# Late attention scores as three 64-row products on the two row halves of TensorE, with ScalarE and VectorE in written order

## The chip, the cores and the metric

The kernel runs on one core of one Trainium2 chip. The metric is the device time of that core in microseconds (us), from start to end of one launch. The time before is 664.21 us, the median of three runs (664.04 to 664.49). One execution was also taken with a profile; the rows shown below are from that execution.

## What is computed

Attention with a banded and a global part, and then a two-layer block that works on each token. There are 4 batches, 8 heads, 768 positions and 64 elements per head. A query looks at the 96 keys that end at itself and at the first 8 keys of the sequence; both limits come as inputs.

```python
scores = scale * np.matmul(q, k.transpose(0, 1, 3, 2))
...
scores = scores + bias[None, :, :, :]          # -slope of the head times distance
scores = np.where(keep, scores, -1000000000.0)
scores = scores - np.max(scores, axis=-1, keepdims=True)
a = np.exp(scores)
a = a / (np.sum(a, axis=-1, keepdims=True) + 1e-09)
return np.matmul(a, v).astype(np.float32)
...
h = x @ w_in                                   # 3072 x 512 by 512 x 2048
relu6 = np.clip(h + 3.0, 0.0, 6.0)
g = h * relu6 / 6.0
return (g @ w_out).astype(np.float32)
```

## The kernel before, in words

**Blocks, pairs, tiles.** The 3,072 tokens are cut into 8 blocks of 384 (two to a batch). A block has 3 tiles of 128 queries, and its 8 heads are handled as 4 pairs. For a tile only 232 keys matter (96 before the tile, 8 global ones, the 128 of the tile); the first tile of a sequence has 128. The attention of the first three blocks (12 pairs, `EARLY`) is done ahead, in an early part; from block 2 of the second layer on, the attention of block i+1 is woven into the two-layer work of block i. "Late" means those 5 blocks, 20 pairs and 60 tiles.

**The two-layer block.** It is done in three products of rounded parts: a high and a low part of each operand, in a 32-bit matmul type of one pass (`F32R`), leaving out low times low. Per step `f` (16 to a block) `first` (L179) issues 12 products of 384 columns, `gate` makes g (ScalarE L190, VectorE L191), `high` rounds it (GpSimd L197 in the late part), `rest` makes the low part (VectorE L204), and `second` (L211) issues 9 products of 512 columns for the step before. `halves` (L448) yields once after each `first` and once after each `second`, so a block has 32 places, called units here, at which attention work is put in. Even units lie behind `first` and `gate`, odd units behind `second`.

**A late pair before.** `attention` (L630) fills the units. Counted from the pair's first unit: units 0, 1 and 2 hold the scores of tiles 0, 1 and 2; unit 3 the first step of `split` for the pair after it, `sum_up` and `normalize` of tiles 0 and 1; unit 4 `normalize` of tile 2, `spread` of tile 0 and the second step of `split`; unit 5 the last two `spread`, `fetch` and the third step of `split`. A pair takes 6 units. After every second pair, at its unit 11, `values` (L917) is issued for both pairs.

- `split` (L783) makes the parts of queries and keys. For each head, q is loaded on both row halves; ScalarE makes the high part q1 (L797), VectorE the low part q2 (L801); GpSimd writes the high part of k on the head's own half (L798) and VectorE the low part of k on the other half (L804). So a tile `kx` holds high over low on 128 rows.
- `scores` (L809) issues for each head two products of 128 rows (L827), q1 on kx and q2 on kx: four products to a tile, into one PSUM bank. In the early part (`plain`, L823) the two heads stand on the two row halves, each with products of 64 rows, and each head has a bank of its own.
- `score` (L841, VectorE) adds distances and takes the minimum; `weigh` (L848, ScalarE) makes exponentials and sums; `sum_up` (L855, L856) and `normalize` (L865, GpSimd) divide.
- `spread` (L890) turns 32 x 32 blocks on VectorE and writes them to DRAM (L892), `fetch` (L899) reads them back turned, both on SyncE's queue. `values` multiplies the weights by v in products with 64 columns of the array (L917).

**What sets the order.** TensorE, SyncE and GpSimd are held in the written order to the end (`in_order`, L565). ScalarE and VectorE are held in it through the early part alone (L541); in the late part the framework's scheduler orders them, by a model of times of its own.

**Memory.** `load` (L298) brings keys and queries of a pair in one transfer and its values in another, into two rooms used in turn. The late scores take their banks in turn from two pools (`bank`, L241).

**The end.** `doubt` (L335) reduces the least scores on VectorE, transposes the result on TensorE (L342) and sets a flag; it is put at unit 4 of the last block.

Of the kernel before, what the change touches and what calls it, by code (L numbers as in the profile page):

```python
# [9 lines left out]
F32 = mybir.dt.float32  # L10
F32R = mybir.dt.float32r
I32 = mybir.dt.int32
U32 = mybir.dt.uint32
AF = mybir.ActivationFunctionType
ALU = mybir.AluOpType
PSUM = bass.MemoryType.PSUM

B, H, S, D = 4, 8, 768, 64
DM, DF = 512, 2048
P = 128  # L20
NT = 3
TB = NT * P
# [11 lines left out]
QW = 2 * TB  # L34
VW = 2 * NT * P
LOAD = KW + QW + VW
# [8 lines left out]
BOTH = EARLY  # L45
# [15 lines left out]
class Kernel:  # L61
# [36 lines left out]
    def constants(self):  # L98
        nc = self.nc
        self.const = self.pool("const", 1)  # L100
        self.ident = self.const.tile([P, P], F32, name="ident")
        make_identity(nc, self.ident)
        self.small = self.const.tile([P, 3], F32, name="small")
        self.little = self.const.tile([P, 2 * NT], F32, name="little")
        nc.vector.memset(self.little, 1e-9)
        self.three = self.small[:, 0:1]
        nc.vector.memset(self.three, 3.0)
# [126 lines left out]
    def attending(self, ctx, heads, rows, ps, **kw):  # L234

        if heads:
            self.hp = self.pool("hp", heads, ctx=ctx, **kw)
        self.up = self.pool("up", rows, ctx=ctx, **kw)
        self.tp = self.pool("tp", ps, ctx=ctx, **kw)
# [58 lines left out]
    def load(self, n, values):  # L298

        if n < len(self.blocks) * NPAIR:  # L300
            end = KW + (TB if n < BOTH else QW)
            for columns in (slice(KW + QW, LOAD),) if values else (slice(0, KW), slice(KW, end)) if n == 0 else (slice(0, end),):
                self.nc.sync.dma_start(out=self.place(n)[:, columns], in_=self.pairs[n, :, columns])
# [8 lines left out]
    def loaded(self, n):  # L312


        at = self.place(n)
        q = at[:, KW:KW + QW].rearrange("p (j t c) -> p j t c", j=2, t=NT)
        v = at[:, KW + QW:LOAD].rearrange("p (s t c) -> p s t c", s=2, t=NT)
        return at[:, 0:KW], q, v[:, 0], v[:, 1]
# [15 lines left out]

    def doubt(self, flag):  # L335


        nc = self.nc
        one = self.small[:, 2:3]
        nc.vector.tensor_reduce(out=one, in_=self.least, op=ALU.max, axis=mybir.AxisListType.X)  # L340
        row = self.bank("t")
        nc.tensor.transpose(row[0:1, 0:P], one, self.ident)  # L342
        top = self.small[0:1, 1:2]
        nc.vector.tensor_reduce(out=top, in_=row[0:1, 0:P], op=ALU.max, axis=mybir.AxisListType.X)
        nc.vector.tensor_scalar(out=flag, in0=top, scalar1=LOW, scalar2=self.beyond(), op0=ALU.is_ge, op1=ALU.max)
# [148 lines left out]
    def banded(self, flag):  # L494
# [12 lines left out]
        with ExitStack() as early, ExitStack() as words:  # L507
# [11 lines left out]
            with ExitStack() as ctx:  # L519
                self.room += self.rooms(self.pool("more", 1, ctx=ctx), MORE - ROOMS, ROOMS)  # L520
                self.load(2, False)
                for n in range(ROOMS):
                    self.load(n, True)
                self.plain_distances(ctx)
                self.attending(ctx, 0, 9, 5)
                pairs = [Pair(self, n, xs[n // NPAIR], True) for n in range(EARLY)]
                todo = self.halves([(0, f, xs[0], acc) for f in range(FIRST)])
                for n in range(-2, EARLY + 1):
                    self.ahead(n, pairs, acc, todo)
                for _ in todo:  # L530
                    pass
# [9 lines left out]
            self.in_order(start, mybir.EngineType.Activation, mybir.EngineType.DVE)  # L541
        self.attending(self.ctx, 2, 3, 2, side="right")
        self.bp = self.pool("bp", 2, side="right")
        self.there = self.pool("there", 2, bass.MemoryType.DRAM)
        self.score_banks = 2
        self.op = self.pool("op", 3, side="right")
        x, ahead = xs[2], None
        for i in range(2, len(self.blocks)):
            units, x_next = [], None
            if i + 1 < len(self.blocks):  # L550
                x_next = self.x_tiles()
                units, ahead = self.attention(i + 1, x_next, ahead)
                if i == 2:
                    units = [[]] + units
            else:
                units = [[]] * 4 + [[lambda: self.doubt(flag)]]
            acc = self.acc_tiles()
            steps = [(i, f, x, acc) for f in range(NF)]
            for k, _ in enumerate(self.halves(steps if x_next else steps[:-3], True)):
                for unit in units[k] if k < len(units) else ():  # L560
                    unit()
            if not x_next:
                self.end(steps[-3:])
            x = x_next
        self.in_order(start, mybir.EngineType.PE, mybir.EngineType.SP, mybir.EngineType.Pool)  # L565
# [64 lines left out]
    def attention(self, i, x, first):  # L630
# [8 lines left out]
        for p in range(NPAIR):  # L639
# [4 lines left out]
            for t in range(NT):  # L644
                at[t].append(lambda t=t, me=me: me.scores(t)())
            if after:
                at[3].append(lambda after=after: after.split(0))
            at[3] += [me.sum_up, lambda me=me: me.normalize(0), lambda me=me: me.normalize(1)]
            at[4] += [lambda me=me: me.normalize(2), lambda me=me: me.spread(0)]
            at[5] += [lambda me=me: me.spread(1), lambda me=me: me.spread(2), me.fetch]  # L650
            for t in range(1, NT if after else 0):
                at[t + 3].append(lambda t=t, after=after: after.split(t))
            if p % 2 == 1:
                at[11] += [lambda me=pairs[p - 1]: me.values("x"), lambda me=me: me.values("s")]
# [113 lines left out]
class Pair:  # L768
# [4 lines left out]
    def __init__(self, kernel, n, x, plain):  # L773
        self.k, self.nc, self.n, self.x, self.plain, self.both = kernel, kernel.nc, n, x, plain, n < BOTH
# [3 lines left out]
        self.parts = [{}, {}]  # L778
# [4 lines left out]
    def split(self, step, load=True):  # L783
# [5 lines left out]
        for j, part in enumerate(self.parts):  # L789
            h = 2 * self.pr + j  # L790
            scale = float(-1.0 / (np.sqrt(D) * SLOPES[h]))
            own, other = (slice(0, D), slice(D, P)) if j == 0 else (slice(D, P), slice(0, D))
            if step == 0:
                part["q1"] = kk.hp.tile([P, NT, P], F32R, name="q1")
                part["q2"] = kk.hp.tile([P, NT, P], F32R, name="q2")
                part["kx"] = kk.hp.tile([P, KW], F32R, name="kx")
                nc.scalar.mul(out=part["q1"], in_=q[:, j], mul=scale)  # L797
                nc.gpsimd.tensor_scalar(out=part["kx"][own, c], in0=k[own, c], scalar1=1.0, scalar2=0.0,  # L798
                                        op0=ALU.mult, op1=ALU.add)
            elif step == 1:  # L800
                nc.vector.scalar_tensor_tensor(out=part["q2"], in0=q[:, j], scalar=scale, in1=part["q1"].bitcast(F32),  # L801
                                               op0=ALU.mult, op1=ALU.subtract)
            else:
                nc.vector.tensor_tensor(out=part["kx"][other, c], in0=k[own, c], in1=part["kx"][own, c].bitcast(F32),  # L804
                                        op=ALU.subtract)
        if step == 2 and load:
            kk.load_next(self.n, False)

    def scores(self, t):  # L809
# [3 lines left out]
        if t != 1 or not self.both:  # L813
            self.banks = [kk.bank("s")[:, 0:2 * W].rearrange("p (i c) -> p i c", i=2) for _ in range(2 if self.both else 1)]
        sp = [self.banks[j][:, t % 2] if self.both else self.banks[0][:, j] for j in range(2)]
# [4 lines left out]
        for j in range(2):  # L820
            if self.plain:
                rows, q = (slice(j * D, (j + 1) * D), 0) if self.both else (slice(None), j)
                nc.tensor.matmul(sp[j][:, lo:W], lhsT=queries[rows, q, t], rhs=keys[rows, c], start=True, stop=True)  # L823
            else:
                part = self.parts[j]
                for m, q in enumerate((part["q1"], part["q2"])):
                    nc.tensor.matmul(sp[j][:, lo:W], lhsT=q[:, t], rhs=part["kx"][:, c], start=(m == 0), stop=(m == 1))  # L827
# [113 lines left out]
def pair_loads(q, k, v):  # L941
# [8 lines left out]
    for b in range(B):  # L950
        for a in range(0, S, TB):
            cols = np.concatenate([np.arange(a - PREV, a).clip(0)]
                                  + [np.concatenate([np.arange(NG), np.arange(p, p + P)]) for p in range(a, a + TB, P)])
            for h in range(0, H, 2):
# [3 lines left out]
                for j in range(2):  # L958
                    for half in range(2):
                        if n >= EARLY or half == j:  # L960
                            column = KW + (j * TB if n >= BOTH else 0)
                            at[half * D:(half + 1) * D, column:column + TB] = qt[j, :, a:a + TB]
                vt = v[b, h:h + 2].transpose(1, 0, 2).reshape(S, P)
                va = at[:, KW + QW:].reshape(P, 2, NT, P)
# [3 lines left out]
                at[:, KW + QW:] = va.reshape(P, VW)  # L968
# [31 lines left out]
```

## Time and profile before

| | |
|---|---|
| median of three runs | 664.21 us |
| profiled execution | 664.76 us |
| its span, first to last instruction | 662.9 us |
| mean granted TensorE clock | 0.999 |
| TensorE busy | 652.2 us, 98% |
| VectorE, ScalarE, GpSimd busy | 402.6, 271.8, 231.5 us |
| late part, 202 to 600 us | TensorE busy 397.63 of 398.00 us |

PE is the row of matmuls and PEld that of weight loads, which run beside the matmuls. The time of a matmul in the trace runs to its modelled end, while the next one has already begun; what a product takes from TensorE is therefore read as the distance from its start to the next start. In the chain of waits, each piece of the span is put down to the work that held up the end. A row of the timeline has the start, the length of the piece, engine, line, operation, output and inputs, shape (rows x columns of the array used, then rows x moving columns) and the count of like instructions that were merged.

### The profile page before, as it was taken

Reading aid. Unit: us, or ns where it says so; the run is one execution under the profiler, and the core shown is the slowest. Engines: PE = TensorE matmul, PEld = TensorE weight load, DVE = VectorE, ACT = ScalarE, POOL = GpSimd, SP = SyncE. Lnnn points to the kernel's source line nnn. Section 1 sums busy time; section 2 is a strip of 40 time slices with the busy share of each in tenths; the row PEclk is TensorE's granted clock in tenths of the full one; section 3 lists DMA queues with packets and bytes.
Section 4 is the critical chain, followed back from the end, with each engine's and each line's share of the span. In section 5 each row is a group of like instructions: output and inputs, shape, how many; then the busy total and the mean of one; then the engine's idle time right before and its main releaser. Section 6 shows DMA issues by size and latency. Waiting matters only on the chain.

```text
span 662.9 us, 11223 instructions
## 1 busy us (share of the span) xinstructions
PE 652.2 (98%) x3963; PEld 582.1 (88%) x3963; DVE 402.6 (61%) x1028; ACT 271.8 (41%) x702; POOL 231.5 (35%) x389
## 2 busy tenths in 40 slices
PE   9989999999999999999999999999999999999997
PEld 8767888888889999899989989899998989989995
DVE  6887677777745776367654777357663677432222
ACT  6998545444445343244314333143422444121111
POOL 4787333333202533034331454134340444312110
PEclk9999999999999999999999999999999999999999
DMA  7975433333003566526652456615654256510001
GB/s 237 314 240 186 150 128 126 120 119 117 29 1 135 147 168 172 149 88 163 172 150 96 122 149 183 176 55 143 163 140 127 88 146 155 130 48 2 0 1 53
DMA packets 58530, 84.32 MB, mean 127 GB/s; under 512 B 8160, under 2 KB 45280, under 8 KB 56416
## 3 DMA queue, kind: packets, MB, share of 16 engines
q1 hardware_dynamic: 58176, 83.25, 42.2%
q8 instruction: 33, 0.54, 0.3%
q14 instruction: 33, 0.27, 0.1%
q10 hardware_dynamic: 288, 0.26, 0.1%
HBM read 62.52 MB, written 20.97 MB: 126 GB/s over the span
## 4 chain that ended last, share of the span: by engine, by line
PE 92%; ACT 4%; DMA 2%; issue 1%; DVE 0%; POOL 0%; SPq 0%; POOLq 0%; ACTq 0%
PE hp L179 40%; PE acc L211 34%; PE xp L917 3%; ACT n L848 2%; PE sp L827 2%; PE sp L211 2%; PE tp L917 2%; PE tp L211 2%; PE xp L211 2%; PE tp L827 2%; PE xp L371 1%; DMA there<-blocks 1%; ACT pt L877 1%; PE sp L823 1%; DMA weights<-there 1%
## 5 line engine op out<-in xcount | busy, mean ns | idle before, releaser
L190 ACT ACTIVATE g<-hp,small 128x384 f32<-128x384 f32 x127 | 73.6, 580 | 254.2 <-PE hp L179 225.8
L179 PE MATMUL hp<-xh,w1h 128*128 128x384 f32 x512 | 173.5, 339 | 0.3 <-DVE pt L877 0.3
L179 PE MATMUL hp<-xh,w1l 128*128 128x384 f32 x512 | 172.6, 337 | 0.0
L179 PE MATMUL hp<-xl,w1h 128*128 128x384 f32 x512 | 171.9, 336 | 0.0
L197 POOL TENSOR_SCALAR gh<-g 128x384 fp32r<-128x384 f32 x96 | 51.6, 537 | 293.9 <-DVE g L191 259.4
L211 PE MATMUL acc<-w2h,gl 128*128 128x512 f32 x336 | 132.8, 395 | 0.0
L211 PE MATMUL acc<-w2h,gh 128*128 128x512 f32 x336 | 132.2, 394 | 0.1
L211 PE MATMUL acc<-w2l,gh 128*128 128x512 f32 x336 | 132.1, 393 | 0.0
L191 DVE SCALAR_TENSOR_TENSOR g<-g,hp 128x384 f32<-128x384 f32 x128 | 69.8, 545 | 85.1 <-ACT g L190 84.7
L204 DVE TENSOR_TENSOR gl<-g,gh 128x384 fp32r<-128x384 f32 x128 | 77.9, 609 | 67.4 <-POOL gh L197 45.3
L865 POOL TENSOR_SCALAR n<-n,sums 128x232 f32<-128x232 f32 (+1 forms) x186 | 99.2, 549 | 28.2 <-DVE sums L856 13.5
L848 ACT ACTIVATE n<-n,least 128x232 f32<-128x232 f32 (+1 forms) x192 | 89.0, 466 | 42.5 <-DVE least L841 41.9
L179 PEld LDWEIGHTS hp<-xh,w1h 128*128 128x128 f32 x512 | 96.3, 188 | 6.1 <-issue 1.5
L179 PEld LDWEIGHTS hp<-xl,w1h 128*128 128x128 f32 x512 | 96.2, 188 | 3.9
L179 PEld LDWEIGHTS hp<-xh,w1l 128*128 128x128 f32 x512 | 96.1, 188 | 0.0
L211 PEld LDWEIGHTS acc<-w2h,gl 128*128 128x128 f32 x336 | 63.0, 188 | 14.6 <-DVE gl L204 0.6
L211 PEld LDWEIGHTS acc<-w2h,gh 128*128 128x128 f32 x336 | 63.3, 188 | 10.6 <-POOL gh L197 0.6
L211 PEld LDWEIGHTS acc<-w2l,gh 128*128 128x128 f32 x336 | 63.2, 188 | 10.2
L890 DVE STREAM_TRANSPOSE blocks<-n 128x256 f32<-128x256 f32 x112 | 43.5, 424 | 31.4 <-POOL n L865 18.6
L385 POOL TENSOR_SCALAR wst<-wst 128x1024 f32<-128x1024 int32 x16 | 23.7, 1480 | 54.6 <-ACT wz L384 54.5
L841 DVE CUSTOM_DVE_ANT_0 n<-sp,d 128x232 f32<-128x232 f32 (+1 forms) x70 | 23.6, 374 | 30.3 <-PE sp L827 29.1
L798 POOL TENSOR_SCALAR kx<-load 64x504 fp32r<-64x504 f32 (+1 forms) x40 | 31.1, 777 | 19.2 <-PE hp L179 17.6
(116 smaller groups left out, 764.1 us busy)
## 6 DMA issues: line engine op xcount, KB each, us to landing
wst<-w SPq DMA_DIRECT2D x16, 1024.0 KB, 4.8
there<-blocks SPq DMA_DIRECT2D x52, 256.0 KB, 2.6
load<-pairs SPq DMA_DIRECT2D x20, 636.0 KB, 5.2
load<-pairs SPq DMA_DIRECT2D x32, 384.0 KB, 4.3
weights<-there SPq DMA_DIRECT2D x48, 192.0 KB, 3.5
out<-o SPq DMA_DIRECT2D x23, 256.0 KB, 2.2
weights<-there SPq DMA_DIRECT2D x32, 160.0 KB, 3.2
load<-pairs SPq DMA_DIRECT2D x11, 444.0 KB, 4.5
```

What stands on the lines that cost most here:

```text
L179: self.nc.tensor.matmul(hp, lhsT=self.w1(w, f)[:, kt, :], rhs=a[:, kt, :], start=(n == 0), stop=(n == 3 * NKT - 1))
L190: nc.scalar.activation(out=g, in_=hp, func=AF.Relu, bias=self.three, scale=1.0)
L191: nc.vector.scalar_tensor_tensor(out=g, in0=g, scalar=6.0, in1=hp, op0=ALU.min, op1=ALU.mult)
L197: self.nc.gpsimd.tensor_scalar(out=gh, in0=g, scalar1=1.0, scalar2=0.0, op0=ALU.mult, op1=ALU.add)
L204: self.nc.vector.tensor_tensor(out=gl, in0=g, in1=gh.bitcast(F32), op=ALU.subtract)
L211: self.nc.tensor.matmul(acc[tt], lhsT=a[:, tk], rhs=self.w2(w, f), start=(f == 0 and j == 0), stop=(f == NF - 1 and j == 2))
L798: nc.gpsimd.tensor_scalar(out=part["kx"][own, c], in0=k[own, c], scalar1=1.0, scalar2=0.0, op0=ALU.mult, op1=ALU.add)
L827: nc.tensor.matmul(sp[j][:, lo:W], lhsT=q[:, t], rhs=part["kx"][:, c], start=(m == 0), stop=(m == 1))
L848: nc.scalar.activation(out=e[:, j, lo:W], in_=e[:, j, lo:W], func=AF.Exp, bias=self.least[:, i:i + 1], scale=-1.0, accum_out=self.sums[:, ...
L865: nc.gpsimd.tensor_scalar(out=e[:, j, lo:W], in0=e[:, j, lo:W], scalar1=over, scalar2=0.0, op0=ALU.mult, op1=ALU.add)
L890: nc.vector.transpose(out=blocks[:, :, s].rearrange("p b j q -> p j b q"), in_=e[:, :, c:c + P].rearrange("p j (b q) -> p j b q", b=4))
L917: nc.tensor.matmul(xps[j * D:(j + 1) * D, t * P:(t + 1) * P], lhsT=vt[0:K, t, j * D:(j + 1) * D], rhs=self.part(t, j, c, K), start=(c == 0 ...
```

## The change

Both heads of a late pair now stand on the two row halves, as in the early part. q and k are each loaded once; `split` makes q1, q2, k1, k2 with one instruction each over all 128 rows, with a column of factors per pair instead of a number per head. `scores` issues three products per head (q1 k1, q1 k2, q2 k1), each of 64 rows, alternating between the halves, so six products to a tile. Each head has its own bank, shared by tiles 0 and 1. The scores of tiles 0 and 1 are issued together in unit 0, and those of tile 2 in unit 2. The steps of `split` move to units 1, 2 and 3, all of `normalize` goes to unit 3, `values` moves from unit 11 to unit 10. The pool of split parts now holds two pairs. In block 2 the attention starts one unit later. The reduction of `doubt` becomes `worst`, two units ahead of the rest, which moves to unit 6. ScalarE and VectorE are held in the written order to the end.

```diff
-        self.attending(self.ctx, 2, 3, 2, side="right")
+        self.op = self.pool("op", 3, side="right")
+        for h in range(H):
+            self.nc.gpsimd.memset(self.factors[h % 2 * D:(h % 2 + 1) * D, h // 2:h // 2 + 1], float(PLAIN / SLOPES[h]))
+        self.attending(self.ctx, 3, 2, side="right")
         self.bp = self.pool("bp", 2, side="right")
+        self.hp = self.pool("hp", 2, side="right")
...
                 if i == 2:
-                    units = [[]] + units
+                    units = [[], []] + units
             else:
-                units = [[]] * 4 + [[lambda: self.doubt(flag)]]
+                units = [[]] * 4 + [[self.worst], [], [lambda: self.doubt(flag)]]
...
-        self.in_order(start, mybir.EngineType.PE, mybir.EngineType.SP, mybir.EngineType.Pool)
+        self.in_order(start, *(getattr(mybir.EngineType, e) for e in ('PE', 'SP', 'Pool', 'Activation', 'DVE')))
...
-            for t in range(NT):
-                at[t].append(lambda t=t, me=me: me.scores(t)())
+            at[0].append(lambda me=me: [f() for f in [me.scores(0), me.scores(1)]])
             if after:
-                at[3].append(lambda after=after: after.split(0))
-            at[3] += [me.sum_up, lambda me=me: me.normalize(0), lambda me=me: me.normalize(1)]
-            at[4] += [lambda me=me: me.normalize(2), lambda me=me: me.spread(0)]
-            at[5] += [lambda me=me: me.spread(1), lambda me=me: me.spread(2), me.fetch]
-            for t in range(1, NT if after else 0):
-                at[t + 3].append(lambda t=t, after=after: after.split(t))
+                at[1].append(lambda after=after: after.split(0))
+            at[2].append(lambda me=me: me.scores(2)())
+            if after:
+                at[2].append(lambda after=after: after.split(1))
+            at[3].append(me.sum_up)
+            at[3].append(lambda me=me: me.normalize(0))
+            at[3].append(lambda me=me: me.normalize(1))
+            at[3].append(lambda me=me: me.normalize(2))
+            if after:
+                at[3].append(lambda after=after: after.split(2))
+            at[4].append(lambda me=me: me.spread(0))
+            at[5].append(lambda me=me: me.spread(1))
+            at[5].append(lambda me=me: me.spread(2))
+            at[5].append(me.fetch)
             if p % 2 == 1:
-                at[11] += [lambda me=pairs[p - 1]: me.values("x"), lambda me=me: me.values("s")]
+                at[10] += [lambda me=pairs[p - 1]: me.values("x"), lambda me=me: me.values("s")]
...
+        factor = kk.factors[:, self.pr:self.pr + 1]
+        if step == 0:
+            self.q1, self.q2 = (kk.hp.tile([P, NT, P], F32R, name=name) for name in ("q1", "q2"))
+            self.k1, self.k2 = (kk.hp.tile([P, KW], F32R, name=name) for name in ("k1", "k2"))
+            nc.scalar.activation(out=self.q1, in_=q, func=AF.Copy, scale=factor)
+            nc.gpsimd.tensor_scalar(out=self.k1[:, c], in0=k[:, c], scalar1=1.0, scalar2=0.0, op0=ALU.mult, op1=ALU.add)
+        elif step == 1:
+            nc.vector.scalar_tensor_tensor(out=self.q2, in0=q, scalar=factor, in1=self.q1.bitcast(F32), op0=ALU.mult, op1=ALU.subtract)
+        else:
+            nc.vector.tensor_tensor(out=self.k2[:, c], in0=k[:, c], in1=self.k1[:, c].bitcast(F32), op=ALU.subtract)
...
-        for j in range(2):
-            if self.plain:
-                rows, q = (slice(j * D, (j + 1) * D), 0) if self.both else (slice(None), j)
-                nc.tensor.matmul(sp[j][:, lo:W], lhsT=queries[rows, q, t], rhs=keys[rows, c], start=True, stop=True)
-            else:
-                part = self.parts[j]
-                for m, q in enumerate((part["q1"], part["q2"])):
-                    nc.tensor.matmul(sp[j][:, lo:W], lhsT=q[:, t], rhs=part["kx"][:, c], start=(m == 0), stop=(m == 1))
+        products = ((queries, keys),) if self.plain else ((self.q1, self.k1), (self.q1, self.k2), (self.q2, self.k1))
+        for m, (q, k) in enumerate(products):
+            for j in range(2):
+                rows = slice(j * D, (j + 1) * D)
+                nc.tensor.matmul(sp[j][:, lo:W], lhsT=q[rows, t], rhs=k[rows, c], start=(m == 0), stop=(m == len(products) - 1))
```

More of the change, by code (lines that the diff above doesn't have):

```diff
@@ L33 @@
 KW = PREV + NT * TG
-QW = 2 * TB
 VW = 2 * NT * P
-LOAD = KW + QW + VW
+LOAD = KW + TB + VW
 NEG = 1.0e9
@@ L44 @@
 EARLY = AHEAD * NPAIR
-BOTH = EARLY
 ROOMS = 2
@@ L103, in constants @@
         self.small = self.const.tile([P, 3], F32, name="small")
+        self.factors = self.const.tile([P, NPAIR], F32, name="factors")
         self.little = self.const.tile([P, 2 * NT], F32, name="little")
@@ L231, in acc_tiles, with attending @@
         return [self.ps_o.tile([P, BANK], F32, name="acc") for _ in range(NT)]
-    def attending(self, ctx, heads, rows, ps, **kw):
-        if heads:
-            self.hp = self.pool("hp", heads, ctx=ctx, **kw)
+    def attending(self, ctx, rows, ps, **kw):
         self.up = self.pool("up", rows, ctx=ctx, **kw)
@@ L300, in load @@
         if n < len(self.blocks) * NPAIR:
-            end = KW + (TB if n < BOTH else QW)
-            for columns in (slice(KW + QW, LOAD),) if values else (slice(0, KW), slice(KW, end)) if n == 0 else (slice(0, end),):
+            end = KW + TB
+            for columns in (slice(end, LOAD),) if values else (slice(0, KW), slice(KW, end)) if n == 0 else (slice(0, end),):
                 self.nc.sync.dma_start(out=self.place(n)[:, columns], in_=self.pairs[n, :, columns])
@@ L315, in loaded @@
         at = self.place(n)
-        q = at[:, KW:KW + QW].rearrange("p (j t c) -> p j t c", j=2, t=NT)
-        v = at[:, KW + QW:LOAD].rearrange("p (s t c) -> p s t c", s=2, t=NT)
+        q = at[:, KW:KW + TB].rearrange("p (t c) -> p t c", t=NT)
+        v = at[:, KW + TB:LOAD].rearrange("p (s t c) -> p s t c", s=2, t=NT)
         return at[:, 0:KW], q, v[:, 0], v[:, 1]
@@ L333, in distances, with worst @@
                     self.nc.gpsimd.tensor_scalar(out=p[:, h], in0=d, scalar1=c, scalar2=0.0, op0=ALU.mult, op1=ALU.add)
+    def worst(self):
+        self.nc.vector.tensor_reduce(out=self.small[:, 2:3], in_=self.least, op=ALU.max, axis=mybir.AxisListType.X)
     def doubt(self, flag):
         nc = self.nc
-        one = self.small[:, 2:3]
-        nc.vector.tensor_reduce(out=one, in_=self.least, op=ALU.max, axis=mybir.AxisListType.X)
         row = self.bank("t")
-        nc.tensor.transpose(row[0:1, 0:P], one, self.ident)
+        nc.tensor.transpose(row[0:1, 0:P], self.small[:, 2:3], self.ident)
         top = self.small[0:1, 1:2]
@@ L524, in banded @@
                 self.plain_distances(ctx)
-                self.attending(ctx, 0, 9, 5)
+                self.attending(ctx, 9, 5)
                 pairs = [Pair(self, n, xs[n // NPAIR], True) for n in range(EARLY)]
@@ L540, in banded @@
                 self.decode_step()
-            self.in_order(start, mybir.EngineType.Activation, mybir.EngineType.DVE)
-        self.attending(self.ctx, 2, 3, 2, side="right")
+        self.op = self.pool("op", 3, side="right")
+        for h in range(H):
+            self.nc.gpsimd.memset(self.factors[h % 2 * D:(h % 2 + 1) * D, h // 2:h // 2 + 1], float(PLAIN / SLOPES[h]))
+        self.attending(self.ctx, 3, 2, side="right")
         self.bp = self.pool("bp", 2, side="right")
+        self.hp = self.pool("hp", 2, side="right")
         self.there = self.pool("there", 2, bass.MemoryType.DRAM)
         self.score_banks = 2
-        self.op = self.pool("op", 3, side="right")
         x, ahead = xs[2], None
@@ L773, in __init__ @@
     def __init__(self, kernel, n, x, plain):
-        self.k, self.nc, self.n, self.x, self.plain, self.both = kernel, kernel.nc, n, x, plain, n < BOTH
+        self.k, self.nc, self.n, self.x, self.plain = kernel, kernel.nc, n, x, plain
         self.tb, self.pr = kernel.blocks[n // NPAIR][1], n % NPAIR
@@ L777, in __init__ @@
         self.sums, self.rows, self.pts = None, [], []
-        self.parts = [{}, {}]
     def low(self, t):
@@ L788, in split @@
         c = slice(CB if self.tb == 0 else 0, None)
[L789 to L802, printed above, removed]
-            else:
[L804 to L807, printed above, removed]
+        factor = kk.factors[:, self.pr:self.pr + 1]
[8 more added lines that the diff above has]
+            nc.vector.tensor_tensor(out=self.k2[:, c], in0=k[:, c], in1=self.k1[:, c].bitcast(F32), op=ALU.subtract)
+            if load:
+                kk.load_next(self.n, False)
     def scores(self, t):
@@ L812, in scores @@
             self.sums = kk.up.tile([P, 2, 2 * NT], F32, name="sums")
-        if t != 1 or not self.both:
-            self.banks = [kk.bank("s")[:, 0:2 * W].rearrange("p (i c) -> p i c", i=2) for _ in range(2 if self.both else 1)]
-        sp = [self.banks[j][:, t % 2] if self.both else self.banks[0][:, j] for j in range(2)]
+        if t != 1:
+            self.banks = [kk.bank("s")[:, 0:2 * W].rearrange("p (i c) -> p i c", i=2) for _ in range(2)]
+        sp = [self.banks[j][:, t % 2] for j in range(2)]
         e = kk.up.tile([P, 2, W], F32, name="n")
@@ L819, in scores @@
         keys, queries, _, _ = kk.loaded(self.n)
-        for j in range(2):
-            if self.plain:
-                rows, q = (slice(j * D, (j + 1) * D), 0) if self.both else (slice(None), j)
-                nc.tensor.matmul(sp[j][:, lo:W], lhsT=queries[rows, q, t], rhs=keys[rows, c], start=True, stop=True)
-            else:
-                part = self.parts[j]
-                for m, q in enumerate((part["q1"], part["q2"])):
-                    nc.tensor.matmul(sp[j][:, lo:W], lhsT=q[:, t], rhs=part["kx"][:, c], start=(m == 0), stop=(m == 1))
+        products = ((queries, keys),) if self.plain else ((self.q1, self.k1), (self.q1, self.k2), (self.q2, self.k1))
[3 more added lines that the diff above has]
+                nc.tensor.matmul(sp[j][:, lo:W], lhsT=q[rows, t], rhs=k[rows, c], start=(m == 0), stop=(m == len(products) - 1))
         self.rows.append(e)
@@ L957, in pair_loads @@
                 at[:, 0:KW] = kt[:, :, cols].reshape(P, KW)
[L958 to L962, printed above, removed]
+                at[:, KW:KW + TB] = qt[:, :, a:a + TB].reshape(P, TB)
                 vt = v[b, h:h + 2].transpose(1, 0, 2).reshape(S, P)
-                va = at[:, KW + QW:].reshape(P, 2, NT, P)
+                va = at[:, KW + TB:].reshape(P, 2, NT, P)
                 va[:, 0] = vt[a:a + TB].reshape(NT, P, P).transpose(1, 0, 2)
@@ L967, in pair_loads @@
                     va[0:CB, 1, t] = vt[tile_rows(a + t * P)]
-                at[:, KW + QW:] = va.reshape(P, VW)
+                at[:, KW + TB:] = va.reshape(P, VW)
                 n += 1
```

## The prediction

> **What bounds the kernel now.** I read the page's first two parts, then the chain of waits, then the busy time by stage, and last the timeline of TensorE where the change cuts in.
>
> ```profile
> span 662.9 us, 11223 instructions
> PE 652.2 (98%) x3963; PEld 582.1 (88%) x3963; DVE 402.6 (61%) x1028; ACT 271.8 (41%) x702; POOL 231.5 (35%) x389
> PEclk9999999999999999999999999999999999999999
> ```
>
> ```profile
> by line: PE hp L179 39.6%; PE acc L211 34.1%; PE xp L917 3.3%; ACT n L848 2.4%; PE sp L827 2.3%; PE sp L211 1.9%; PE tp L917 1.9%; PE tp L211 1.7%; PE xp L211 1.7%; PE tp L827 1.7%; PE xp L371 1.4%; DMA there<-blocks 0.9%; ACT pt L877 0.7%;
> ```
>
> ```profile
> 202.00:600.00 398.00, 397.63 (x2410) 361.01 (x2409) 241.37 (x654) 141.34 (x398) 139.12 (x240) 1.00 0.49 135
> ```
>
> The last row is the late part; its busy times stand in the order PE, PEld, DVE, ACT, POOL. TensorE (PE) is busy for 397.63 of 398.00 us, and the granted clock is full. Nothing else in the late part is on the path: what shortens TensorE's stream shortens the kernel, and what makes TensorE stand longer between two products lengthens it one for one. The late scores (L827) are 2.3% + 1.7% = 4.0% of the chain, 26.5 us. That is all that the change can work on directly.
>
> **What the old scores cost.**
>
> ```profile
> 439.71 0.34 PE L179 MATMUL hp<-xh,w1l 128*128 128x384 f32 x1
> 439.88 0.60 PE L827 MATMUL sp<-kx,q 128*128 128x232 f32 x4
> 440.32 0.40 PE L211 MATMUL acc<-w2h,gh 128*128 128x512 f32 x1
> 440.56 0.39 PE L211 MATMUL acc<-w2l,gh 128*128 128x512 f32 x1
> ```
>
> Read by starts: four products take 440.32 - 439.88 = 0.44 us, 0.11 us each, and the products before and after them run at their usual distance (0.17 us for 384 columns, 0.24 for 512 here). So the scores enter and leave TensorE's stream at no cost. 60 tiles at 0.44 make 26.4 us, which agrees with the chain's 26.5.
>
> **What the new scores stream.** Six products to a tile, but two at a time on the two row halves. The early part already does this, in plain 32-bit products of two passes each:
>
> ```profile
> 32.70 0.27 PE L873 MATMUL hp<-ident,n 128*128 128x128 f32 x1
> 32.81 0.27 PE L875 MATMUL hp<-ident,n 128*128 128x128 f32 x1
> 33.02 0.46 PE L823 MATMUL sp<-load 64*128 64x232 f32 x1
> 33.02 0.46 PE L823 MATMUL acc<-load 64*128 64x232 f32 x1
> 33.32 0.36 PE L823 MATMUL sp<-load 64*128 64x232 f32 x1
> 33.32 0.36 PE L823 MATMUL acc<-load 64*128 64x232 f32 x1
> 33.51 0.36 PE L823 MATMUL sp<-load 64*128 64x232 f32 x1
> 33.52 0.36 PE L823 MATMUL acc<-load 64*128 64x232 f32 x1
> ```
>
> The two halves start at the same moment and the next two follow 0.19 us later, so two products cost one slot. A slot of the new type at 232 columns is not in this trace. Its ends: 0.106 us, if it streams like `second` (one piece of the chain below has nine products of 512 columns in 2.10 us, 0.456 ns to a column), and 0.19 us, if it streams like these plain passes. I take 0.11, the same type and the same number of columns in L827, because what the row half changes is the rows and not the columns; two plain 64-row slots of 128 columns are also 0.11 apart:
>
> ```profile
> 38.35 0.27 PE L823 MATMUL sp<-load 64*128 64x128 f32 x1
> 38.35 0.27 PE L823 MATMUL acc<-load 64*128 64x128 f32 x1
> 38.46 0.36 PE L823 MATMUL sp<-load 64*128 64x232 f32 x1
> ```
>
> ```profile
> 279.75 2.10 PE acc L211 x9
> ```
>
> 60 tiles x 3 slots x 0.11 = 19.8 us. Streaming alone saves 26.5 - 19.8 = 6.7 us.
>
> **What it costs to change the shape.** The rows above also show the entry into row halves. Two 128-row products stand 0.11 apart (32.70, 32.81), but the first 64-row one follows after 0.21: 0.10 lost. Its successor follows after 0.30 instead of 0.19 to 0.20: another 0.10, in which the first weight load is seen unhidden. One entry costs 0.20 us. The way out of a changed shape back into `first` stands behind every `values`, whose products use 64 columns of the array; the way out of row halves stands at 13.68:
>
> ```profile
> 398.76 0.28 PE L917 MATMUL tp<-weights,load 104*64 104x128 f32 x2
> 398.97 0.44 PE L179 MATMUL hp<-xh,w1h 128*128 128x384 f32 x1
> 399.25 0.34 PE L179 MATMUL hp<-xl,w1h 128*128 128x384 f32 x1
> 399.43 0.35 PE L179 MATMUL hp<-xh,w1l 128*128 128x384 f32 x1
> ```
>
> ```profile
> 13.09 0.66 PE L823 MATMUL acc<-load 64*128 64x232 f32 x4
> 13.68 0.33 PE L873 MATMUL tp<-ident,n 128*128 128x128 f32 x1
> ```
>
> `first` begins 0.21 after the last pair of `values` (their slots are 0.11), and its second product follows after 0.28 instead of 0.18: 0.10 + 0.10. From row halves, two slots with the entry's delay would end at 13.09 + 0.30 + 0.19 = 13.58, and the next product starts at 13.68: 0.10 again. So one excursion into row halves and back costs 0.20 + 0.20 = 0.40 us.
>
> The old scores had none of these, since L827 uses the array in the same shape as the two-layer products. The new scores make two excursions per pair: tiles 0 and 1 together in unit 0, tile 2 in unit 2, with `second` and `first` between them. 20 pairs x 2 x 0.40 = 16.0 us. The ends for one excursion are 0.37 and 0.42 (rounding of four starts), so 14.8 to 16.8.
>
> [...]
>
> **The other parts.** Half of the `split` work goes: one instruction per step instead of two.
>
> ```profile
> L798 POOL TENSOR_SCALAR kx<-load 64x504 fp32r<-64x504 f32 (+1 forms) x40 | 31.1, 777 | 19.2 <-PE hp L179 17.6
> L801 DVE SCALAR_TENSOR_TENSOR q<-load,q 128x384 fp32r<-128x384 f32 x40 | 25.1, 667 | 0.1
> L804 DVE TENSOR_TENSOR kx<-load,kx 64x504 fp32r<-64x504 f32 (+1 forms) x40 | 27.1, 677 | 1.2
> ```
>
> That is some 26 us off VectorE and 16 us off GpSimd, with a shorter transfer for q besides, all beside a TensorE that never waits for them: worth nothing. `worst` two units ahead of `doubt`, the eight memsets and the new pool order lie beside TensorE as well: nothing, at most a few tenths of a us either way.
>
> ScalarE and VectorE in written order can cost. Behind `first`, VectorE now has in one row: `gate`, four `score`, `rest`. With 0.55, 4 x 0.47 and 0.61 us, and 0.58 of ScalarE ahead, `gl` is done some 3.6 us after `first` ends. The `second` that reads it starts after the new scores (0.66 + 0.40), another `second` and another `first` (2.1 each), 5.3 us after: 1.7 us to spare. The tightest place is the third `spread`, which reuses a buffer still being written to DRAM, and now holds up `gate` behind it:
>
> ```profile
> DVE blocks L890 <- DMA there<-blocks: 12.7, 11, 2.7
> ```
>
> ```profile
> L191 DVE SCALAR_TENSOR_TENSOR g<-g,hp 128x384 f32<-128x384 f32 x128 | 69.8, 545 | 85.1 <-ACT g L190 84.7
> L204 DVE TENSOR_TENSOR gl<-g,gh 128x384 fp32r<-128x384 f32 x128 | 77.9, 609 | 67.4 <-POOL gh L197 45.3 <-ACT gh L199 22.2
> L841 DVE CUSTOM_DVE_ANT_0 n<-tp,d 128x232 f32<-128x232 f32 (+1 forms) x50 | 17.4, 384 | 7.8 <-PE tp L827 7.6
> ```
>
> A mean wait of 1.2 us fits into the 1.7, the longest (2.7) does not. So the bounds are 0 and 20 x 1.0 = 20 us; I take 0, by the mean. `values` one unit earlier is the other place: one unit is 2.1 us, and its weights come in by a `fetch` that lands shortly before.
>
> ```profile
> 497.01 1.74 SPq L899 DMA_DIRECT2D weights<-there  x4
> 503.39 0.44 PE L917 MATMUL xp<-weights,load 128*64 128x128 f32 x4
> weights<-there SPq DMA_DIRECT2D x48, 192.0 KB, 3.5
> ```
>
> Issued to 498.75 and 3.5 to land, they are there at about 502.2 at the latest, 1.2 us before use. Of the 2.1 us, the earlier `normalize` of tile 2 (no longer behind two L798, 2 x 0.78, and a `gh`) gives back about 1.6, and the excursions of that pair 0.4 to 0.8. I take 0; the bound is 10 places x 0.9 = 9 us.
>
> **The sum.** -6.7 + 16.0 = +9.3 us. On the profiled execution's own time, 664.76, that is 674.1; the median of the runs lies 0.55 lower, so the forecast for the median is **673.5 us**. With the ends of the slot down to 0.106 and of the excursion, the forecast's own range is 671 to 675.
>
> **The rivals.**
>
> [...] If 64-row products of this type went in and out of the stream like L827, only the streaming would be left: 664.2 - 6.7 = 657.5, faster. The point from which it decides is 6.7 / 40 = 0.17 us for an excursion. Against it: of the entries into row halves and the exits into `first` and `second` that I read, none costs less than 0.19. For it: all entries into row halves in this trace are of plain 32-bit products. Chance 0.07. Half of it, 0.20 for an excursion, because the first weight load hides, gives +1.3, 665.5: no change that counts. Chance 0.03.
>
> *Written order adds waits.* If the third `spread` or the earlier `values` holds up TensorE by 0.5 us per pair, 20 x 0.5 = 10 us come on top: 683. Chance 0.11.
>
> *The slots are longer.* If within a half the next weight load can't go on beside the running product, every slot has the 0.10 of the first one: 180 x 0.10 = 18 us on top, 691.5. Against it: 33.32 to 33.51, and the 0.11 behind 38.35, have no such gap. Streaming at the plain rate gives 180 x 0.08 = 14 us on top, 688. Chance of either 0.04.
>
> [...]
>
> **How the numbers follow.** The forecast has 0.75. Two tenths of a per cent, about 1.3 us, is what a measurement of this kernel can tell from no change. Faster by more: 0.07; within: 0.03; slower: 0.75 + 0.11 + 0.04 = 0.90. The range reaches up into the cases with some added waits, to 680, and down to 669, which leaves out the first rival, its half, the longer slots and the worse part of the waits, together about 0.19.
>
> **What would show it.** In the changed profile: score slots 0.11 us apart with both halves starting together (else the slot is wrong); about 0.10 lost ahead of the first score product and 0.10 behind it, and the same at the first `second` or `first` after (else the excursion is wrong); TensorE without waits for `gl`, `gh` or `weights` in the late part (else written order has a price); span longer by about 9 us with the granted clock unchanged. The prediction is wrong if an excursion costs under 0.17 us.

## The result and the profile after

The changed kernel takes 675.37 us (median of six runs, 674.68 to 678.31), the kernel before 664.35 us in the same series: a ratio of 1.0174, 95% interval 1.0154 to 1.0194. The change costs 11.0 us; the forecast was 9.3 more, 673.5 us.

The profiled execution of the changed kernel is the slowest of its six, 678.31 us with a span of 676.5 us, so its span against the 662.9 us of before overstates the loss. A second profile, of an execution of 674.99 us, has a span of 673.1 us (experiment e5 below); comparisons of spans use that one.

The page of the changed kernel: its first lines show more matmuls and less of everything else. VectorE has dropped from 402.6 to 358.4 us of work and GpSimd from 231.5 to 199.3, while TensorE's share stands where it was.

```profile
span 676.5 us, 11327 instructions
PE 663.3 (98%) x4083; PEld 579.2 (86%) x4083; DVE 358.4 (53%) x988; ACT 265.6 (39%) x682; POOL 199.3 (29%) x377
```

The late part of the changed kernel, from the busy times by stage (columns PE, PEld, DVE, ACT, POOL): TensorE is busy for 395.22 of 397.00 us. So 1.8 us of standing still are now to be seen there, where before there were 0.4.

```profile
207.00:604.00 397.00, 395.22 (x2470) 345.35 (x2470) 195.40 (x609) 130.45 (x371) 105.67 (x218) 1.00 0.44 123
```

The timeline of TensorE in the changed kernel at a unit 0, tiles 0 and 1 together:

```profile
535.74 0.34 PE L178 MATMUL hp<-xl,w1h 128*128 128x384 f32 x1
535.91 0.34 PE L178 MATMUL hp<-xh,w1l 128*128 128x384 f32 x1
536.18 0.37 PE L824 MATMUL sp<-k,q 64*128 64x232 f32 x1
536.18 0.37 PE L824 MATMUL tp<-k,q 64*128 64x232 f32 x1
536.39 0.27 PE L824 MATMUL sp<-k,q 64*128 64x232 f32 x1
536.39 0.28 PE L824 MATMUL tp<-k,q 64*128 64x232 f32 x1
536.50 0.27 PE L824 MATMUL sp<-k,q 64*128 64x232 f32 x1
...
536.84 0.27 PE L824 MATMUL sp<-k,q 64*128 64x232 f32 x1
536.84 0.27 PE L824 MATMUL tp<-k,q 64*128 64x232 f32 x1
537.04 0.49 PE L210 MATMUL acc<-w2h,gh 128*128 128x512 f32 x1
537.38 0.39 PE L210 MATMUL acc<-w2l,gh 128*128 128x512 f32 x1
```

Read the starts down the column. Both halves start together, and slots stand 0.11 apart (536.39, 536.50). The first slot begins 0.27 after a product of 384 columns, whose usual distance is 0.17: 0.10 lost. It lasts 0.21 instead of 0.11: 0.10 lost. The first L210 comes 0.20 after the last slot instead of 0.11, and the second one 0.34 after the first instead of 0.23: 0.09 and 0.11 lost. That is one excursion at 0.40 us, in this row as in the early rows that the prediction read.

TensorE's 1.8 us of standing still is one place nearly alone, in the timeline of the changed kernel's profiled execution, where the second half of a `values` waits for the weights that `fetch` brings:

```profile
590.85 1.54 PE L914 MATMUL xp<-weights,load 128*64 128x128 f32 x24
593.76 1.54 PE L914 MATMUL tp<-weights,load 128*64 128x128 f32 x24 [1.37 <-DMA weights<-there]
```

VectorE's and SyncE's timelines of the same execution show what stood ahead of it. The third `spread` of the pair (584.39) waited 3.20 us for its buffer, and `fetch`, which comes behind it, was issued from 587.81 to 589.64, 3.0 us before `values` began:

```profile
580.42 0.76 DVE L887 STREAM_TRANSPOSE blocks<-n 128x256 f32<-128x256 f32 x2
584.39 0.77 DVE L887 STREAM_TRANSPOSE blocks<-n 128x256 f32<-128x256 f32 x2 [3.20 <-DMA there<-blocks]
```

```profile
579.92 5.78 SPq L889 DMA_DIRECT2D there<-blocks  x3
587.81 1.83 SPq L896 DMA_DIRECT2D weights<-there  x4
```

In the table of waits, that wait of `spread` has grown from 12.7 us in 11 places to 29.4 us in 20:

```profile
DVE blocks L887 <- DMA there<-blocks: 29.4, 20, 3.2
```

The length of that wait does not decide by itself: without the written order (e4 below) it is 34.5 us in 16 places, the longest 4.3 us, and TensorE waits for no weights there.

### The profile page after: what moved, and what is told of

It is laid out like the page before. It is cut to its first block, busy times and chain, and to the rows that moved or that the text cites. A ratio compares the mean times of both kernels' runs of the same rounds, so it can differ in the third digit from the quotient of the medians.

```text
span 676.5 us, 11327 instructions
## 1 busy us (share of the span) xinstructions
PE 663.3 (98%) x4083; PEld 579.2 (86%) x4083; DVE 358.4 (53%) x988; ACT 265.6 (39%) x682; POOL 199.3 (29%) x377
## 4 chain that ended last, share of the span: by engine, by line
PE 91%; ACT 4%; DMA 2%; issue 1%; DVE 1%; POOL 0%; SPq 0%; DVEq 0%; ACTq 0%
PE hp L178 39%; PE acc L210 35%; PE sp L824 4%; PE xp L914 3%; ACT n L845 2%; PE sp L210 2%; PE tp L210 2%; PE xp L210 2%; PE tp L824 1%; DMA there<-blocks 1%; PE tp L914 1%; PE xp L370 1%; PE sp L914 1%; ACT pt L874 1%; DMA weights<-there 1%
## 5 line engine op out<-in xcount | busy, mean ns | idle before, releaser
L196 POOL TENSOR_SCALAR gh<-g 128x384 fp32r<-128x384 f32 x96 | 49.2, 513 | 334.9 <-DVE g L190 319.0
L210 PE MATMUL acc<-w2h,gh 128*128 128x512 f32 x336 | 136.9, 407 | 0.0
L210 PE MATMUL acc<-w2h,gl 128*128 128x512 f32 x336 | 132.8, 395 | 0.2 <-DVE gl L203 0.2
L210 PE MATMUL acc<-w2l,gh 128*128 128x512 f32 x336 | 132.2, 394 | 0.0
L862 POOL TENSOR_SCALAR n<-n,sums 128x232 f32<-128x232 f32 (+1 forms) x186 | 88.2, 491 | 40.9 <-DVE sums L853 29.9
L203 DVE TENSOR_TENSOR gl<-g,gh 128x384 fp32r<-128x384 f32 x128 | 71.7, 560 | 47.6 <-POOL gh L196 24.1
L210 PEld LDWEIGHTS acc<-w2h,gh 128*128 128x128 f32 x336 | 63.1, 188 | 16.7 <-issue 1.7
L210 PEld LDWEIGHTS acc<-w2h,gl 128*128 128x128 f32 x336 | 63.1, 188 | 14.9 <-DVE gl L203 1.2
L210 PEld LDWEIGHTS acc<-w2l,gh 128*128 128x128 f32 x336 | 63.2, 188 | 10.0
L887 DVE STREAM_TRANSPOSE blocks<-n 128x256 f32<-128x256 f32 x112 | 43.3, 422 | 29.4 <-DMA there<-blocks 29.4
L845 ACT ACTIVATION_READ_ACCUMULATOR n<-n,least 128x1 f32 x192 | 36.1, 188 | 0.0
L824 PE MATMUL tp<-k,q 64*128 64x232 f32 (+1 forms) x180 | 30.5, 294 | 0.0
```

The lines of the kernel that those rows point to most:

```text
L196: self.nc.gpsimd.tensor_scalar(out=gh, in0=g, scalar1=1.0, scalar2=0.0, op0=ALU.mult, op1=ALU.add)
L203: self.nc.vector.tensor_tensor(out=gl, in0=g, in1=gh.bitcast(F32), op=ALU.subtract)
L210: self.nc.tensor.matmul(acc[tt], lhsT=a[:, tk], rhs=self.w2(w, f), start=(f == 0 and j == 0), stop=(f == NF - 1 and j == 2))
L824: nc.tensor.matmul(sp[j][:, lo:W], lhsT=q[rows, t], rhs=k[rows, c], start=(m == 0), stop=(m == len(products) - 1))
L845: nc.scalar.activation(out=e[:, j, lo:W], in_=e[:, j, lo:W], func=AF.Exp, bias=self.least[:, i:i + 1], scale=-1.0, accum_out=self.sums[:, ...
L862: nc.gpsimd.tensor_scalar(out=e[:, j, lo:W], in0=e[:, j, lo:W], scalar1=over, scalar2=0.0, op0=ALU.mult, op1=ALU.add)
```

## The experiments

Two series, each on one chip, with the kernel before timed beside them (663.75 us in the first, 663.95 us in the second). "Above" means above that.

| run | median us | above | span of its profile |
|---|---|---|---|
| e1, one tile per excursion (60) | 681.90 | 18.2 | 680.8 |
| e2, the change without its products | 691.37 | 27.6 | 689.3 |
| e3, before with 40 excursions added | 681.32 | 17.6 | 679.3 |
| e4, the change, ScalarE and VectorE free | 672.80 | 9.1 | 670.9 |
| e5, the change again | 676.43 | 12.5 | 673.1 |
| e6, the change, values at unit 11 | 673.37 | 9.4 | 671.6 |
| e7, e4 with one excursion per pair (20) | 666.09 | 2.1 | 665.2 |
| e8, before in written order | 713.97 | 50.0 | 711.3 |

**What an excursion costs.** The theory: each time TensorE goes into row halves and back costs 0.40 us, whatever it does there. Rivals: the slots are longer, or the written order and the earlier `values` took the time.

e1 undoes "tiles 0 and 1 together":

```diff
-            at[0].append(lambda me=me: [f() for f in [me.scores(0), me.scores(1)]])
+            at[0].append(lambda me=me: me.scores(0)())
+            at[1].append(lambda me=me: me.scores(1)())
```

> The changed kernel with one tile of scores per unit (units 0, 1, 2), so three excursions into row halves per pair instead of two; the products are the same. Theory (an excursion costs TensorE 0.40 us whatever it carries): 20 more excursions, +8.0 us on the changed kernel's 675.4, so 683.4, and 19.0 us above the kernel before. Rival (the time was lost to the written order, the earlier values, or longer slots): within 1 us of 675.4.

Measured: 681.90 us, ratio 1.0275 (1.0256 to 1.0295). Its span is 7.7 us over that of e5, which is 0.38 us for each of the 20 excursions added; but e5's profiled execution is its fastest, and that of e1 lies 0.7 us above its median. The medians give 5.7 to 7.1 us, 0.28 to 0.36 each, since the changed kernel's own runs scatter. The rival's "within 1 us" is out.

e3 adds the excursions to the kernel before and nothing else:

```diff
+        if not self.plain and t != 1:
+            idle = kk.bank("x")
+            part = self.parts[0]
+            nc.tensor.matmul(idle[:, 0:P], lhsT=part["q1"][0:D, t], rhs=part["kx"][0:D, CB:CB + P], start=True, stop=True)
```

> The kernel before with one extra 64-row product of 128 columns behind the scores of tiles 0 and 2 of each late pair, written to the free bank and read by nobody: 40 excursions and 40 slots added, nothing else changed (this adds work that the result does not use). Theory: 40 x (0.40 + 0.11) = 20.4 us, 684.8. [...]

Measured: 681.32 us, ratio 1.0267 (1.0250 to 1.0284), 17.6 us above; 20.4 was expected, and the added products' slots alone, 40 x 0.11, are 4.4. The timeline of e3 around one of them:

```profile
415.30 0.60 PE L827 MATMUL sp<-kx,q 128*128 128x232 f32 x4
415.84 0.33 PE L831 MATMUL xp<-kx,q 64*128 64x128 f32 x1
416.09 0.50 PE L211 MATMUL acc<-w2h,gh 128*128 128x512 f32 x1
416.43 0.40 PE L211 MATMUL acc<-w2l,gh 128*128 128x512 f32 x1
```

Four L827 at 0.11 should end at 415.74; the added product starts at 415.84, 0.10 late. It holds TensorE for 0.25, and the second L211 comes 0.34 after the first instead of 0.23. With 0.10 before, 0.11 behind, and 0.20 of the 0.25 as in the changed kernel's rows, 0.05 is left for the product, not the 0.11 that I had put in. 40 x (0.40 + 0.05) = 18.0, against 17.6. This split is an account and not a measurement. In a row of slots a 128-column product takes 0.11, as the changed kernel shows where the first tile of a sequence has 128 columns (one of the two halves):

```profile
283.34 0.27 PE L824 MATMUL sp<-k,q 64*128 64x128 f32 x1
283.45 0.27 PE L824 MATMUL sp<-k,q 64*128 64x128 f32 x1
283.56 0.32 PE L824 MATMUL sp<-k,q 64*128 64x232 f32 x1
```

Counted at 0.11, the 0.44 us that each addition cost leaves 0.33 for the excursion, and counted at 0.05 it leaves 0.39. One 64-row product by itself, in one half, costs the whole excursion (17.6 / 40 = 0.44 us each, product included); two halves in flight are not needed for it. No run adds the same product with 128 rows; that such a product would cost no more than its slot is read from the L827 rows before, four in 0.44 us with no time lost on either side (439.88 to 440.32), and is my estimate.

e7 goes the other way, with all three tiles in unit 0. The third tile takes the bank of `values` for one head and a bank of the first layer for the other:

```diff
-            at[0].append(lambda me=me: [f() for f in [me.scores(0), me.scores(1)]])
+            at[0].append(lambda me=me: [f() for f in [me.scores(t) for t in range(NT)]])
-            at[2].append(lambda me=me: me.scores(2)())
...
-            self.banks = [kk.bank("s")[:, 0:2 * W].rearrange("p (i c) -> p i c", i=2) for _ in range(2)]
+            two = [kk.bank("s"), kk.bank("s")] if self.plain or t == 0 else [kk.bank("x"), kk.ps_h.tile([P, BANK], F32, name="hp")]
+            self.banks = [bank[:, 0:2 * W].rearrange("p (i c) -> p i c", i=2) for bank in two]
```

> The kernel with ScalarE and VectorE free in the late part (673 us in the run before), with all three tiles of a pair in unit 0, the third in the bank of the values and one of the two banks of the first layer: one excursion per pair, 20 in all instead of 40. Theory (0.40 us an excursion): 8 us less than that kernel, so about 1 us above the kernel before. Rival (the cost goes with the products and not with the excursions): no change from 673.

Measured: 666.09 us, ratio 1.0030 (1.0018 to 1.0043): 6.7 us less than e4 by the medians, 5.7 by the spans, of 8 expected. Its table of waits shows where one us of the rest is: TensorE waited once for the low part of g, which stood on VectorE behind a `spread` that had waited 2.88 us for its buffer.

```profile
PE acc L210 <- DVE gl L203: 1.1, 1, 1.1
```

```profile
416.25 0.77 DVE L888 STREAM_TRANSPOSE blocks<-n 128x256 f32<-128x256 f32 x2 [2.88 <-DMA there<-blocks]
416.95 0.52 DVE L203 TENSOR_TENSOR gl<-g,gh 128x384 fp32r<-128x384 f32 x1
```

```profile
417.52 0.50 PE L210 MATMUL acc<-w2h,gl 128*128 128x512 f32 x1 [1.08 <-DVE gl L203]
```

With that us added back, the spans give 6.8 / 20 = 0.34 us for an excursion.

So 20 and 40 excursions stand at 2.1 and 9.1 us above the kernel before with ScalarE and VectorE free (e7, e4), and 40 and 60 at 11.0 to 12.5 and 18.2 us in written order, with the same products. Three rows of products on row halves would pay only below 6.7 / 0.40 = 17 excursions for 20 pairs; with the scores in four banks, one pair to an excursion is the least that I found room for. No version here beats the kernel before.

**What the order costs.** e4 takes the written order of ScalarE and VectorE away again in the late part:

```diff
+        self.in_order(start, mybir.EngineType.Activation, mybir.EngineType.DVE)
...
-        self.in_order(start, *(getattr(mybir.EngineType, e) for e in ('PE', 'SP', 'Pool', 'Activation', 'DVE')))
+        self.in_order(start, *(getattr(mybir.EngineType, e) for e in ('PE', 'SP', 'Pool')))
```

> The changed kernel with ScalarE and VectorE held in written order through the early part alone, as before the change. Theory (the order is hidden beside TensorE but for the wait of the values for their weights): 675.4, at most 1.5 us less. Rival (the written order is what costs): 668 or less.

Measured: 672.80 us, ratio 1.0139 (1.0122 to 1.0156), 9.1 us above. The shape of the products is most of the loss, and the written order costs 2.0 to 3.4 us on top (11.0 and 12.5 less 9.1; by the spans of e5 and e4, 2.2): more than the 1.5 that I had allowed. The traces show one way. In the three places where e5's `values` wait, `fetch` was issued 4.4, 4.6 and 4.0 us before they began; in the same places of e4 it was 5.4, 5.5 and 4.8 us, and TensorE did not wait at all in the late part.

e5 is the change again, unedited, beside e6 with one line changed:

```diff
-                at[10] += [lambda me=pairs[p - 1]: me.values("x"), lambda me=me: me.values("s")]
+                at[11] += [lambda me=pairs[p - 1]: me.values("x"), lambda me=me: me.values("s")]
```

> The changed kernel itself, unedited, timed and profiled beside the three below. Theory (8 to 9 us from the shape of the products, about 2 us from the written order, of which most is the values waiting for their weights): 10 to 11 us above the kernel before, and in its trace a wait of 1 to 2 us of the values in the block before the last. Rival (the first run's profile had a chance event, and the written order costs nothing): 8 to 9 us above, no such wait.

> The changed kernel with the values back at unit 11, all else as changed. Theory (the written order costs through the wait for the fetched weights): 1 to 1.8 us less than the changed kernel, and no wait for weights in its trace. Rival (the written order costs through gate, rest and the end of the kernel): the same time as the changed kernel within 0.5 us.

Measured: e5 676.43 us (1.0174 to 1.0213), 12.5 above; e6 673.37 us (1.0126 to 1.0160), 9.4 above. e5 lies above the 10 to 11 us that I had expected. In its table of waits the weights hold up `values` in three places, the one in the block before the last with 0.6 us, where I had expected 1 to 2:

```profile
PE tp L914 <- DMA weights<-there: 1.1, 3, 0.6
```

In e6 there is no such row. So the waits of the weights go with the unit, and the median with them (3.1 us, more than the 1.1 us that e5's profiled execution shows, but that execution was the fastest of e5's four). The three kernels with the written order and `values` at unit 10 scatter widely: 674.68 to 678.31 and 674.99 to 677.74 for the change, 681.05 to 683.52 for e1, while e4 and e6 stay within 0.7 us. That would fit a wait for the weights that differs from run to run (1.6 us in the change's first profile, 1.1 in e5's), but it is not shown. e7, with no wait for weights in its profile, scatters from 665.05 to 667.20, and the kernel before from 663.31 to 665.37 in the same series; and most of the difference between the two profiled executions of the change arose at their start (last section).

What e6 keeps over e4, 0.6 us, has a place too. In the changed kernel, and in e6 alike, VectorE's order now puts `doubt` ahead of `gl`, and the flag waits for nine small GpSimd steps (L251 to L256):

```profile
617.54 0.27 DVE L343 TENSOR_REDUCE small<-tp 1x1 f32<-1x128 f32 x1
620.62 0.20 DVE L344 TENSOR_SCALAR flag<-small,iv 1x1 int32<-1x1 f32 x1 [2.80 <-POOL iv L256]
620.75 0.54 DVE L203 TENSOR_TENSOR gl<-g,gh 128x384 fp32r<-128x384 f32 x1
```

```profile
620.76 0.40 PE L210 MATMUL acc<-w2l,gh 128*128 128x512 f32 x1
621.34 0.51 PE L210 MATMUL acc<-w2h,gl 128*128 128x512 f32 x1 [0.18 <-DVE gl L203]
621.68 0.40 PE L210 MATMUL acc<-w2h,gh 128*128 128x512 f32 x1
```

The product that reads `gl` starts 0.58 after the one before it instead of 0.23, and the next one 0.34 after it: about 0.46 us.

e2 and e8 ask what the written order costs without the rest of the change. e8 is the kernel before with that alone:

```diff
-            self.in_order(start, mybir.EngineType.Activation, mybir.EngineType.DVE)
...
-        self.in_order(start, mybir.EngineType.PE, mybir.EngineType.SP, mybir.EngineType.Pool)
+        self.in_order(start, *(getattr(mybir.EngineType, e) for e in ('PE', 'SP', 'Pool', 'Activation', 'DVE')))
```

> The kernel before with ScalarE and VectorE in written order to the end and nothing else changed. Theory (the written order alone is nearly hidden; the 27 us of the old products in the new places came from the values a unit earlier behind the larger split): 0 to 3 us above the kernel before. Rival (the written order itself is the large price when VectorE has the old, double split): 10 us or more above, with TensorE waits for kx or for weights.

e2 is the kernel before in the new places, and in written order as well; the lines that do the latter, and those for `worst` and for block 2 one unit later, are left out here:

```diff
...
+            at[0].append(lambda me=me: [f() for f in [me.scores(0), me.scores(1)]])
+            at[2].append(lambda me=me: me.scores(2)())
+            for k in range(3 if after else 0):
+                at[k + 3].append(lambda k=k, after=after: after.split(k))
+            at[3] += [me.sum_up] + [lambda t=t, me=me: me.normalize(t) for t in range(NT)]
+            at[4].append(lambda me=me: me.spread(0))
             at[5] += [lambda me=me: me.spread(1), lambda me=me: me.spread(2), me.fetch]
...
             if p % 2 == 1:
-                at[11] += [lambda me=pairs[p - 1]: me.values("x"), lambda me=me: me.values("s")]
+                at[10] += [lambda me=pairs[p - 1]: me.values("x"), lambda me=me: me.values("s")]
```

> The kernel before with all of the change but its products: four 128-row products to a tile and the old split (at units 3, 4, 5, since only one pair of split parts fits), with tiles 0 and 1 together, all of normalize at unit 3, values at unit 10, the worst reduction apart, block 2 one unit later and ScalarE and VectorE in written order. Theory (only the products' shape matters): 664.4, within 1 us of the kernel before. Rival (the written order and the earlier values carry a good part of the 11 us): 667 or more, with TensorE waits in its trace for gl, gh or the fetched weights.

Both of my expectations were far off. e8: 713.97 us, ratio 1.0759 (1.0738 to 1.0781), 50.0 above. e2: 691.37 us, ratio 1.0420 (1.0402 to 1.0438), 27.6 above. The tables of waits say why; first e8, then e2:

```profile
PE sp L826 <- DVE kx L803: 17.0, 20, 3.3
PE tp L826 <- DVE kx L803: 10.8, 9, 3.3
```

```profile
PE tp L917 <- DMA weights<-there: 12.0, 8, 2.9
PE tp L827 <- DVE kx L804: 1.8, 8, 0.3
PE sp L827 <- DVE kx L804: 1.7, 8, 0.3
```

In e8's written order the last step of `split` stands behind the `spread` steps of unit 5, and the scores of unit 6 wait for it, 28 us of them in sum. In e2 it stands ahead of the last two `spread`, and then `spread`, `fetch` and `values` are late. The waits are not the whole price. The mean granted clock, 0.999 before, is 0.985 in e8 and 0.993 in e2. In e8's chain of waits six pieces of nine or twelve products took 3.06 to 3.60 us, where the others listed of that many took 2.11 to 2.36; at the end of one of the six, 512-column products stand 0.43 us apart (329.56, 329.99), against 0.23 at 333.99 and 334.22. The clock's share is an estimate: 0.014 of the span of 711.3 us, about 10 us. Why the granted clock is lower there no run shows. The rival was right here: the written order is a large price where `split` stands close to its use. In the changed kernel it is small, and there `split` is done in units 1 to 3, three units ahead of the scores, with half the instructions. That these two are what makes it small follows from the waits; it was not tried by moving `split` alone.

## Why the prediction was right, and where it was off

- **The slot**, 0.11 us: right (536.39 to 536.50). It streams like the old products, not like the plain ones at 0.19. The rival of the longer slots is out: the changed kernel's trace has 360 weight loads for these 360 products, and the slots behind the first stand 0.11 apart all the same (536.39 to 536.84). A slot of 128 columns takes 0.11 as well (283.34 to 283.45), so the number of columns is not what sets its length there.
- **The excursion**, 0.40 us: right in where the time is lost, 0.10 and 0.10 us on the way in and 0.09 and 0.11 on the way out, and by these four distances in its size; what TensorE does in that time no run shows. By time it comes out at or below that: 0.28 to 0.38 from e1, 0.33 or 0.39 from e3, 0.34 from e7.
- **The sum of both**, +9.3 us: e4, which has the new products without the written order, is 9.1 us above by its median, and its trace has no wait of TensorE in the late part.
- **"ScalarE and VectorE in written order ... I take 0"** and **"`values` one unit earlier ... I take 0"**: the terms that were mis-sized. Together they cost 2.0 to 3.4 us by the medians. The prediction named both places, the third `spread` and the `fetch`, but took the first for a danger to `gate` and `gl` and worked out a margin for the second apart from it. In the changed kernel's two traces no `spread` made TensorE wait for `gl` (in e7 one did, for 1.1 us); what reached TensorE were the weights, since `spread` and with it `fetch` come later in the written order. Neither term costs more than some tenths by itself: `values` at unit 10 in free order (e4) is 9.1 us above, the written order with `values` at unit 11 (e6) 9.4. What share of the 2.0 to 3.4 us is the waits alone stays open; e5's profile shows 1.1 us of them.
- **"`worst` ... nothing, at most a few tenths"**: 0.46 us, by another way than I looked for: in written order the flag stands ahead of `gl`.
- **The chances**: the forecast's own range, 671 to 675, misses the median by 0.4 us; the full range holds it.

## What to carry to other kernels

On a saturated TensorE, count the changes of array shape as you count columns: here a trip into row halves and back costs as much as 3 to 3.6 slots (0.33 to 0.40 us over 0.11), so cutting four slots to three pays only if many tiles share one trip. Price a hand-written order by what it makes late in turn, and not by the waits on an engine that has time: here the longest waits of `spread` stand in the free order, which cost TensorE no wait in e4. Before a difference between two executions is put down to a step, look where in time it arises.

## What the runs showed that I had not expected

- The written order, alone and on the kernel before, costs 50.0 us (e8), the lost clock (about 10 us by the estimate above) included. The scheduler's own order avoided that much.
- At the start of the changed kernel's profiled execution, ten small 128-column products (L370) took 2.43 us; in e5 the same ten took 1.38, after a wait of the same 0.60 us for the first load. The products behind them start at 10.39 us there and at 8.07 in e5, 2.3 us of the 3.4 by which the two spans differ. The score products ahead of them were slower too: 232-column slots start 0.39 us apart (6.31, 6.70), against 0.20 (5.85, 6.05) in e5. A lower clock would fit that, but it is not shown: the trace's record of the granted clock begins at 10.3 us there, at full clock, and the 1.00 in the rows by stage for the time before has no record behind it. What slowed them is open. First the changed kernel's first profile, then e5:

```profile
5.75 0.55 PE L824 MATMUL sp<-load 64*128 64x128 f32 x1 [0.60 <-DMA load<-pairs]
...
8.03 2.43 PE L370 MATMUL xp<-small 128*128 128x128 f32 x10
```

```profile
5.55 0.34 PE L824 MATMUL sp<-load 64*128 64x128 f32 x1 [0.60 <-DMA load<-pairs]
...
6.76 1.38 PE L370 MATMUL xp<-small 128*128 128x128 f32 x10
```
